# VectorE's side work in the attention takes one input from PSUM, and the PSUM banks are shared out anew

## The chip, the cores and the metric

The kernel runs on one core of one Trainium2 chip. The metric is the device time of one execution in microseconds; the median of three executions of the kernel before is 677.43 us.

## The reference

Three stages follow each other. A linear attention with a decayed state gives `x` (3072 tokens of 384); a router gives each token to one of eight experts, 384 tokens each, in the order of the logits over all tokens; each expert is a two-layer net, and its rows go on through a layer with three weights, a maximum over the three products, and an output weight.

```python
for t in range(S):                                   # attention, B=4, H=8, S=768, D=48
    cur = np.einsum('bhd,bhe->bhde', u[None] * kt, vt)
    y[:, :, t] = np.einsum('bhd,bhde->bhe', rt, state + cur)
    state = w[None, :, :, None] * state + np.einsum('bhd,bhe->bhde', kt, vt)
...
for idx in np.argsort(-logits.flatten()):            # routing, logits = x @ w_gate
    tok, e = (int(idx) // E, int(idx) % E)
    if assigned[tok] >= 0 or counts[e] >= cap:
        continue
    assigned[tok] = e
...
out[mask] = np.maximum(x[mask] @ w1[e], 0.0) @ w2[e] # experts
...
h = np.maximum(np.maximum(x @ w1, x @ w2), x @ w3)   # last layer, weights in float64
return (h @ w_out).astype(np.float32)
```

## The kernel before

The attention is cut into 24 steps (`NT`), one for each of 4 batches and 6 chunks of 128 positions; chunks are the outer loop, so the first four steps have no state yet. `Attention.run` writes the order of the work out by hand, and every engine works its instructions off in that order. In step i it issues: loads for steps i+4 and i+3 on SP's queue; on POOL `decayed(i+2)` (L129), `natural(i+3)` (L184), `bonus(i+2)` (L192, L193); a slot of side work; `turn(i+2)`, four TensorE transposes into the PSUM tile `pT`, which ScalarE copies to `kt` (L213, L215); `fade(i-1)`, four ScalarE scalings of the state `S` (L293); a second slot; `scores(i+1)`, sixteen matmuls into two `pA` tiles, masked to `am` by two VectorE products (L227, L230); `extra(i+1)`, a VectorE sum `bon` and a POOL product `bv` (L201, L203); a third slot; `cross(i-1)`, three transposes of `x` into the PSUM tile `pX`, copied to `xt` by ScalarE, and ScalarE's sum of squares of `x` (L302 to L305); `keep(4)`, four matmuls on constants whose result nobody reads (L237, constant `KEEP`); `rows(i)`, the products with the state and with `am` into two `pY` tiles, added to `bv` as `x` by VectorE (L248, L263); `gate(i-2)`, the logits into the bank `lg` (L313); a fourth slot; and `state(i)`, eight products into the PSUM tile `pK`, to which VectorE adds `S` as `st` (L281, L285).

The side work prepares weights for the later stages while the attention runs. `Feed.take` hands it out by slot: each item has a cost, and a slot's budget is what brings the feed up to the share of the whole cost that is due by then, at most 0.9. Three kinds of items matter here.

- `weight`: four sums of squares of a weight's two loaded blocks on ScalarE (`look`, L628), a scale found from them, then `split(n)`: ScalarE writes the scaled weight rounded to f16 (`upper`, L695), and one item later VectorE subtracts this from the scaled weight for the f16 rest (`lower`, L699). In the attention it runs for both weights of expert 0 (six parts of 512 columns, four of 768), and for the first weight of expert 1 without the rests (`left`).
- `double`: decodes a float64 weight in three blocks of 768 columns to f32 in SBUF. ScalarE writes the magnitude into `da` (L745), VectorE shifts it (`shift`, L760), joins low bits (`low`, L767) and the sign (`sign`, L776), ScalarE squares the result (L628), and after the scale is known `split(j)` halves it as above (ScalarE L801, VectorE L804). It runs for two of the three weights.
- `spread`: the peak over partitions: a transpose of one column (`turn`, L410) in slot 4, a VectorE maximum (L412), a matmul that hands it to all partitions (`share`, L416) in slot 2 of the next step, and five small VectorE operations on it. Both use a fresh `pX`.

The eight PSUM banks are: `lg` 1, `pX` 1, `pT` 1, `pA` 2, `pY` 2, `pK` 1.

```python
            side(1)
            self.turn(i + 2)
            self.fade(i - 1)
            side(2)
            self.scores(i + 1)
            self.extra(i + 1)
            side(3)
            if i < NT - 2:
                self.cross(i - 1)
                self.keep(KEEP)
                self.rows(i)
```

Of the kernel before, what the change touches and what calls it, by code (L numbers as in the profile page):

```python
# [18 lines left out]
C = 128  # L19
# [18 lines left out]
KEEP = 4  # L38
# [6 lines left out]
class Attention:  # L45


    def __init__(self, ctx, tc, K, r, rt, k, v, w, u, wg, x_dram, spare, routing):
# [7 lines left out]
        self.psum = ctx.enter_context(tc.tile_pool(name="psum_a", bufs=1, space=PSUM))  # L56
        self.ST = {}
# [38 lines left out]
        self.bank = self.psum.tile([128, 512], F32, name="lg")  # L96
        self.lg = self.bank[:, :NT * E].rearrange("p (m e) -> p m e", e=E)
# [33 lines left out]
    def tables(self, wcol):  # L131
# [27 lines left out]
        idle = psum.tile([128, 512], F32, name="pX")  # L159
# [111 lines left out]
    def state(self, i):  # L271
# [5 lines left out]
        pk = psum.tile([128, NP, WIDE], F32, name="pK")  # L277
# [18 lines left out]
    def cross(self, i):  # L296
# [3 lines left out]
        px = psum.tile([128, 3, C], F32, name="pX")  # L300
# [92 lines left out]
class Scales:  # L393
# [9 lines left out]
    def spread(self, peak, then):  # L403
# [4 lines left out]
        def turn():  # L408
            p = self.psum()
            nc.tensor.transpose(p[:1, :128], peak() if callable(peak) else peak, self.K.identf)  # L410
            st["m"] = self.tile(shape=(1, 1))
            nc.vector.tensor_reduce(st["m"], p[:1, :128], AX.X, OP.max)  # L412

        def share():
            p = self.psum()
            nc.tensor.matmul(p[:, :1], self.K.onesf[:1, :], st["m"], start=True, stop=True)  # L416
            then(p[:, :1])
# [179 lines left out]
class Experts:  # L597
# [27 lines left out]

    def square(self, x, total):
# [27 lines left out]
    def weight(self, e, which, routed=False, left=False):  # L654
# [37 lines left out]

        def upper(n):
            raw, (hi, _) = part(*parts[n])
            nc.scalar.activation(hi, raw, AF.Copy, scale=st["s"])  # L695

        def lower(n):
            raw, (hi, lo) = part(*parts[n])
            nc.vector.scalar_tensor_tensor(lo, raw, st["s"], hi, op0=OP.mult, op1=OP.subtract)  # L699

        def split(n):
            def go():
                if n < len(parts):
                    upper(n)
                if n and not left:
                    lower(n - 1)
            return go
# [19 lines left out]
    def double(self, i):  # L727
# [14 lines left out]
        def magnitude(j):  # L742
            a = bits[j] = self.wp.tile([128, 768], I32, name="da", bufs=2)
            a = a.bitcast(F32)
# [18 lines left out]
        def low(j):  # L763
            def go():
                if j + 1 < nb:
# [32 lines left out]
        def split(j):  # L798
            def go():
                if j < nb:  # L800
                    nc.scalar.activation(halves(j)[0], st["x"][:, j], AF.Copy, scale=st["s"])  # L801
                if j:
                    hi, lo = halves(j - 1)
                    nc.vector.scalar_tensor_tensor(lo, st["x"][:, j - 1], st["s"], hi, op0=OP.mult, op1=OP.subtract)  # L804
            return go

        near = [[blocks[j]] + blocks[j + 1:j + 2] for j in range(nb)]
        return ([(lambda: magnitude(0), False, blocks[:1], 0.3)] * (not early)
                + [(f(j), False, b, t) for j in range(nb)
                   for f, b, t in ((shift, blocks[j:j + 1] if early else near[j], 0.8), (low, near[j], 1.1), (sign, blocks[j:j + 1], 1.1))]  # L810
# [673 lines left out]
def body(ctx, tc, r, rt, k, v, w, u, wg, w1, w2, v1, v2, v3, wo, out, dbg=None):  # L1484
# [14 lines left out]
    with ExitStack() as actx:  # L1499
        A = Attention(actx, tc, K, r, rt, k, v, w, u, wg, x_dram,  # L1500
                      lambda: X.wp.tile([128, 1536], F32, name="stage", bufs=Feed.SLOTS), routing)
        X.sc.psum = lambda: A.psum.tile([128, 3, C], F32, name="pX").rearrange("p j n -> p (j n)")
# [51 lines left out]
```

## Time and profile before

| what | before |
|---|---|
| median of 3 runs (all) | 677.43 us (676.73, 677.43, 841.12) |
| the profiled execution, its own time | 679.12 us |
| span in the profile | 677.4 us |
| busy PE / VectorE / ScalarE / POOL | 95% / 58% / 52% / 35% |
| mean granted TensorE clock | 0.957 |

The time is what a run measures; the span is from the first to the last instruction of the profiled execution. The attention takes the time from about 11 us to 158.7 us, where ScalarE reads the finished logits; routing follows up to about 200 us, and the experts take the rest. Rows of a timeline give the start in us, the time from the first start to the last end of a merged group, engine, line, operation, written tile and read tiles, shape, and the number of instructions; in square brackets stands the idle time of the engine before it and what ended that.

### The profile page before, as it was taken

The numbers are of one execution on the slowest core, as the hardware profiler recorded it, in microseconds if no ns is written. First come the engines' busy times: TensorE is split into PE (matmuls) and PEld (weight loads), VectorE is DVE, ScalarE is ACT, GpSimd is POOL, SyncE is SP. The second block draws the span as 40 slices with busy tenths as digits, with TensorE's granted clock in tenths as the row PEclk, the third lists the DMA queues.
The fourth block names the chain that finished last, engine by engine and source line by source line (L and its number), as shares of the span: only waits on it lengthen the run. The fifth ranks groups of instructions, "written<-read, shape, count | busy, mean of one in ns | idle before, by whom it ended". The sixth has DMA issues, their size and how long they took to land.

```text
span 677.4 us, 14362 instructions
## 1 busy us (share of the span) xinstructions
PE 642.2 (95%) x5660; PEld 429.9 (63%) x5660; DVE 394.8 (58%) x1027; ACT 350.2 (52%) x782; POOL 238.2 (35%) x268
## 2 busy tenths in 40 slices
PE   6999899998779998999999999999999999999996
PEld 4788787887566664666666666656665666666663
DVE  7777988757745767774556366354626544451321
ACT  3567474854443557574755655546544545332321
POOL 6989999980150003231122023112202111110222
PEclk8889998996579999999999999999999999999999
DMA  8877876625054309064134135112414200000000
GB/s 223 291 233 226 292 223 183 210 81 210 2 156 82 142 3 204 28 125 144 59 117 118 47 129 117 48 59 71 117 47 129 53 30 13 24 1 1 36 1 35
DMA packets 54763, 72.98 MB, mean 108 GB/s; under 512 B 21408, under 2 KB 42016, under 8 KB 54688
## 3 DMA queue, kind: packets, MB, share of 16 engines
q1 hardware_dynamic: 51616, 62.55, 31.3%
q0 software_dynamic: 3072, 9.44, 4.8%
q8 instruction: 46, 0.75, 0.5%
q14 instruction: 29, 0.24, 0.1%
HBM read 58.41 MB, written 9.44 MB: 100 GB/s over the span
## 4 chain that ended last, share of the span: by engine, by line
PE 60%; issue 7%; DVE 2%; POOL 1%; ACT 1%; POOLq 0%; DVEq 0%
PE pg L932 29%; PE ps L932 23%; PE px L1027 8%; POOL gt L1014 1%; DVE top L1009 1%; ACT gt L1013 0%; POOL out_dram L1034 0%; PE px L914 0%; POOLq L1550 0%; DVE da L760 0%; ACT top L1007 0%; ACT x2s L989 0%; ACT junk L628 0%; DVE sc L435 0%; DVE xr L905 0%
## 5 line engine op out<-in xcount | busy, mean ns | idle before, releaser
L932 PE MATMUL pg<-x2s,v 128*128 128x384 f16 x1296 | 217.0, 326 | 2.7 <-ACT top L1007 2.7
L932 PEld LDWEIGHTS <-v 128*128 128x128 f16 x1296 | 126.8, 98 | 86.8 <-issue 3.2
L1014 POOL TENSOR_TENSOR gt<-top,gt 128x384 f16<-128x384 f32 x48 | 44.4, 925 | 341.3 <-ACT gt L1013 291.9
L932 PEld LDWEIGHTS <-w 128*128 128x128 f16 x1242 | 117.2, 99 | 73.1 <-issue 1.6
L1009 DVE SCALAR_TENSOR_TENSOR top<-pg,sc,top 128x384 f32<-128x384 f32 x96 | 59.1, 616 | 75.0 <-PE pg L932 66.2
L932 PE MATMUL ps<-ht,w 128*128 128x384 f16 x576 | 94.9, 326 | 0.0
L699 DVE SCALAR_TENSOR_TENSOR w<-stage,sc,w 128x512 f16<-128x512 f32 (+1 forms) x80 | 70.4, 903 | 41.1 <-ACT w L695 40.8
L932 PE MATMUL ps<-xt,w 128*128 128x384 f16 (+1 forms) x540 | 88.6, 317 | 0.2 <-issue 0.2
L1013 ACT ACTIVATE gt<-top 128x384 f16<-128x384 f32 x48 | 25.0, 522 | 111.6 <-DVE top L1009 109.4
L1027 PE MATMUL px<-wo,gt 128*128 128x384 f16 x432 | 72.2, 326 | 1.8 <-POOL spacer L1033 1.0
L695 ACT ACTIVATE w<-stage,sc 128x512 f16<-128x512 f32 (+1 forms) x80 | 62.0, 797 | 3.0 <-DVE sc L466 1.2
L1027 PEld LDWEIGHTS <-gt 128*128 128x128 f16 x432 | 41.9, 98 | 30.8 <-POOL spacer L1033 1.7
L628 ACT ACTIVATE junk<-stage 128x768 bf16<-128x768 f32 x64 | 53.6, 837 | 6.3 <-DMA stage<-in_moe_w_dram 5.6
L962 DVE SCALAR_TENSOR_TENSOR ht<-ps,ht 128x384 f16<-128x384 f32 x56 | 30.9, 555 | 32.0 <-ACT ht L961 31.9
L1034 POOL DMA_INDIRECT out_dram<-o,ids x24 | 23.8, 993 | 40.8 <-ACT o L1032 40.8
L973 ACT ACTIVATE x<-ps 128x384 f32<-128x384 f32 x24 | 11.8, 490 | 49.7 <-PE ps L932 49.7
L230 DVE TENSOR_TENSOR am<-pA,mask 128x512 f32<-128x512 f32 x48 | 30.8, 682 | 10.3 <-PE pA L227 10.2
L1007 ACT ACTIVATE top<-pg,sc 128x384 f32<-128x384 f32 x48 | 27.7, 576 | 17.6 <-PE pg L932 17.2
L961 ACT ACTIVATE ht<-ps 128x384 f16<-128x384 f32 x56 | 26.7, 481 | 16.1 <-PE ps L932 16.0
L129 POOL TENSOR_TENSOR rt<-rt,tr 128x512 f32<-128x512 f32 x22 | 31.6, 1438 | 1.3 <-DMA rt<-in_rt_dram 1.3
L227 PE MATMUL pA<-rt,kt 64*128 64x128 f32 x384 | 29.9, 295 | 2.0 <-DVE am L230 1.9
L184 POOL TENSOR_TENSOR kp<-kn,tkn 128x384 f32<-128x384 f32 (+1 forms) x25 | 28.3, 1135 | 4.4 <-ACT tkn L168 3.8
(238 smaller groups left out, 851.9 us busy)
## 6 DMA issues: line engine op xcount, KB each, us to landing
stage<-in_moe_w_dram SPq DMA_DIRECT2D x41, 768.0 KB, 5.2
kn<-in_k_dram SPq DMA_DIRECT2D x24, 192.0 KB, 5.0
rn<-in_r_dram SPq DMA_DIRECT2D x24, 192.0 KB, 5.4
v<-in_v_dram SPq DMA_DIRECT2D x24, 192.0 KB, 3.2
rt<-in_rt_dram SPq DMA_DIRECT2D x48, 96.0 KB, 3.5
x_rows<-x SPq DMA_DIRECT2D x24, 192.0 KB, 2.6
stage<-in_moe_w_out_dram SPq DMA_DIRECT2D x3, 768.0 KB, 6.3
xg<-x_rows,ids POOLq DMA_INDIRECT x24, 5.1
```

The source lines that it names most:

```text
L129: (engine or self.nc.gpsimd).tensor_mul(self.RT[i], self.RT[i], self.tr)
L184: self.nc.gpsimd.tensor_mul(self.KN[i][:, heads, :D], kn[:, heads], self.tkn[:, heads, :D])
L227: nc.tensor.matmul(pa[s][:, j, :], kt[FULL[s], j * C:(j + 1) * C], rt[FULL[s], j * C:(j + 1) * C], start=True, stop=True, skip_group_check ...
L230: nc.vector.tensor_mul(am[:, s], pa[s], self.mask[:, None, :].to_broadcast([128, NP, C]))
L628: self.nc.scalar.activation(self.K.junk, x, AF.Square, accum_out=total)
L695: nc.scalar.activation(hi, raw, AF.Copy, scale=st["s"])
L699: nc.vector.scalar_tensor_tensor(lo, raw, st["s"], hi, op0=OP.mult, op1=OP.subtract)
L932: nc.tensor.matmul(p[:, rows], w[:, wi, k, cols], x[:, xi, k, rows], start=k == 0 and wi + xi == 0, stop=k == kb - 1 and xi == 1, skip_gro ...
L962: nc.vector.scalar_tensor_tensor(h[:, 1, f], p, 0.0, h[:, 0, f], op0=OP.max, op1=OP.subtract)
L1009: nc.vector.scalar_tensor_tensor(t, p, self.ratio[i], top, op0=OP.mult, op1=OP.max)
L1014: nc.gpsimd.tensor_sub(gt[:, 1, g], top, gt[:, 0, g])
L1027: nc.tensor.matmul(p, gt[:, gi, g, a * 128:(a + 1) * 128], self.WO[:, wi, g, :], start=g == 0 and gi + wi == 0, stop=g == self.KG - 1 and ...
```

## The change

- A PSUM tile `lane` of two banks is set up once. The bank of `pX` is gone, and the tile `pK` moves into the upper half of the bank `lg` (columns 256 to 511), so that logits, state products, the matmuls of `keep` and, in columns 192 to 255, the result of `share` stand in one bank.
- `cross` and the transpose of `spread` use `pT`, the tile of `turn`. There is one buffer of it.
- In `weight` (not for the `left` one) and in `double`, ScalarE copies each upper half from SBUF (f16) into `lane` (f32) after it has written it, and VectorE's subtraction reads it there. Parts of up to 512 columns take the two banks of `lane` in turn; parts of 768 columns all use the same 768 columns.
- The magnitudes of blocks 1 and 2 of each `double` are written to `lane` in place of SBUF, and shifted, joined and read there. ScalarE's magnitude of the next block is an item of its own (cost 0.3) behind the sign of the block ahead; before, it was issued together with `low` of the block ahead, into another buffer.
- `KEEP` goes from 4 to 2.

```diff
-KEEP = 4
+KEEP = 2
...
+        self.lane = self.psum.tile([128, 1024], F32, name="lane")
...
+        self.spot = self.bank[:, 192:256]
+        self.pk = self.bank[:, 256:].rearrange("p (j n) -> p j n", n=WIDE)
...
-        idle = psum.tile([128, 512], F32, name="pX")
+        idle = self.lane[:, 512:]
...
-        pk = psum.tile([128, NP, WIDE], F32, name="pK")
+        pk = self.pk
...
-        px = psum.tile([128, 3, C], F32, name="pX")
+        px = psum.tile([128, 512], F32, name="pT")[:, :DM].rearrange("p (j n) -> p j n", n=C)
...
         def turn():
-            p = self.psum()
+            p = self.row()
...
         def share():
-            p = self.psum()
+            p = self.spot()
...
+    def twin(self, n, width):
+
+        n = n % 2 * 512 if width <= 512 else 0
+        return self.lane[:, n:n + width]
...
+        apart = self.early and not left
+
+        def copy(n):
+            raw, (hi, _) = part(*parts[n])
+            nc.scalar.activation(self.twin(n, raw.shape[-1]), hi, AF.Copy)
+
         def lower(n):
             raw, (hi, lo) = part(*parts[n])
+            if apart:
+                hi = self.twin(n, raw.shape[-1])
             nc.vector.scalar_tensor_tensor(lo, raw, st["s"], hi, op0=OP.mult, op1=OP.subtract)
...
                 if n and not left:
                     lower(n - 1)
+                if n < len(parts) and apart:
+                    copy(n)
...
         def magnitude(j):
-            a = bits[j] = self.wp.tile([128, 768], I32, name="da", bufs=2)
-            a = a.bitcast(F32)
+            if early and j:
+                a = self.lane[:, :768]
+                bits[j] = a.bitcast(I32)
+            else:
+                bits[j] = self.wp.tile([128, 768], I32, name="da", bufs=2)
+                a = bits[j].bitcast(F32)
...
         def low(j):
             def go():
-                if j + 1 < nb:
+                if j + 1 < nb and not early:
                     magnitude(j + 1)
...
                 if j:
                     hi, lo = halves(j - 1)
+                    if early:
+                        hi = self.twin(0, 768)
                     nc.vector.scalar_tensor_tensor(lo, st["x"][:, j - 1], st["s"], hi, op0=OP.mult, op1=OP.subtract)
+                if j < nb and early:
+                    nc.scalar.activation(self.twin(0, 768), halves(j)[0], AF.Copy)
...
+                   for f, b, t in [(size, near[j], 0.3)] * (early and j > 0)
+                   + [(shift, near[j], 0.8), (low, near[j], 1.1), (sign, blocks[j:j + 1], 1.1)]]
...
+        X.sc.row, X.sc.spot, X.lane = lambda: A.psum.tile([128, 512], F32, name="pT"), lambda: A.spot, A.lane
```

On ScalarE, where the first `double`'s result is split (`v` is the f16 weight, `kt` and `xt` the copies of `turn` and `cross`), the kernel before has:

```order
L801 ACTIVATE v_82<-wo,sc_1626 128x768 [waits DVE_49]
L304 ACTIVATE xt<-pX 128x384 [waits PE_49]
L305 ACTIVATE junk,norms<-x 128x384 [waits Activation_49]
L801 ACTIVATE v_82<-wo,sc_1626 128x768 x2
L215 ACTIVATE kt_111<-pT 128x512 [waits PE_49]
```

The changed kernel has at the same place:

```order
L823 ACTIVATE v_82<-wo,sc_1593 128x768 [waits DVE_49]
L830 ACTIVATE lane<-v_82 128x768 [waits Activation_49]
L307 ACTIVATE xt<-pT 128x384 [waits PE_49]
L308 ACTIVATE junk,norms<-x 128x384
L823 ACTIVATE v_82<-wo,sc_1593 128x768
L830 ACTIVATE lane<-v_82 128x768 [waits DVE_49,Activation_49]
L823 ACTIVATE v_82<-wo,sc_1593 128x768
L830 ACTIVATE lane<-v_82 128x768 [waits DVE_49,Activation_49]
L218 ACTIVATE kt_112<-pT 128x512 [waits PE_49]
```

Three copies into `lane` have come in ahead of `kt`, and the second and third wait for VectorE. The order of VectorE at this place is the same in both kernels but for the operand:

```order
L266 TENSOR_TENSOR x<-pY,bv 128x4x48 [waits DMAHW2_49,PE_49,Pool_49]
L266 TENSOR_TENSOR x<-pY,bv 128x4x48 [waits PE_49]
...
L828 SCALAR_TENSOR_TENSOR v_82<-wo,sc_1593,lane 128x768 [waits DVE_49,Activation_49]
L288 TENSOR_TENSOR st<-lg,S_117 128x192 [waits PE_49]
L828 SCALAR_TENSOR_TENSOR v_82<-wo,sc_1593,lane 128x768 [waits Activation_49] x2
L233 TENSOR_TENSOR am<-pA,mask 128x512 [waits PE_49] x2
```

The subtraction stands behind `x`, `st` and ahead of `am`, and now reads `lane`.

On TensorE, the kernel before has in one step of the steady part:

```order
L213 MATMUL pT<-identf,kp_115 128x128 [waits Activation_49,Pool_49]
L213 MATMUL pT<-identf,kp_115 128x128 x3
...
L302 MATMUL pX<-identf,x 128x128 [waits DVE_49,Activation_49]
L302 MATMUL pX<-identf,x 128x128 x2
L237 LDWEIGHTS onesf
L237 MATMUL lg<-onesf 128x256
L237 LDWEIGHTS onesf
L237 MATMUL lg<-onesf 128x256
```

and the changed kernel:

```order
L216 MATMUL pT<-identf,kp_114 128x128 [waits Activation_49,Pool_49]
L216 MATMUL pT<-identf,kp_114 128x128 x3
...
L305 MATMUL pT<-identf,x 128x128 [waits DVE_49,Activation_49]
L305 MATMUL pT<-identf,x 128x128 x2
L240 LDWEIGHTS onesf
L240 MATMUL lg<-onesf 128x256 [waits DVE_49]
```

Both kinds of transposes now write `pT`, so that the wait of `cross` for ScalarE is one for the `kt` copy of the same step, and that of `turn` one for the `xt` copy of the step ahead; before, each waited for the copy of its own tile one step earlier. The matmuls of `keep` wait for VectorE's `st`, which reads their bank.

## Rows read from the trace of the kernel before

**Rows 1.** Windows: TensorE, weight loads, VectorE, ScalarE, POOL busy (instructions), clock, DMA share, GB/s.

```profile
80.00:100.00 20.00, 19.53 (x410) 16.71 (x407) 17.70 (x34) 14.17 (x39) 19.76 (x16) 1.00 0.75 241
```

**Rows 2.** Timeline of one step of the attention, TensorE and ScalarE.

```profile
64.03 0.69 PE L281 MATMUL pK<-v,kp 128*64 128x64 f32 x16
...
64.64 0.66 PE L213 MATMUL pT<-identf,kp 128*128 128x128 f32 x4
...
65.33 0.60 ACT L215 ACTIVATE kt<-pT 128x512 f32<-128x512 f32 x1 [0.96 <-PE pT L213]
...
65.83 1.00 ACT L293 ACTIVATE S<-st,w 128x48 f32<-128x48 f32 x4
...
66.32 0.55 PE L302 MATMUL pX<-identf,x 128*128 128x128 f32 x3
...
66.70 0.60 PE L237 MATMUL lg<-onesf 128*128 128x256 bf16 x4
...
67.23 0.69 PE L248 MATMUL pY<-S,rt 64*64 64x64 f32 x32
...
68.94 0.83 PE L313 MATMUL lg<-wg,xt 128*128 128x8 f32 x6
...
69.70 0.69 PE L281 MATMUL pK<-v,kp 128*64 128x64 f32 x16
```

**Rows 3.** Timeline of POOL: two successive products `rt`, twice.

```profile
65.92 1.98 POOL L129 TENSOR_TENSOR rt<-rt,tr 128x512 f32<-128x512 f32 x1
...
73.69 1.58 POOL L129 TENSOR_TENSOR rt<-rt,tr 128x512 f32<-128x512 f32 x1
...
141.58 1.27 POOL L129 TENSOR_TENSOR rt<-rt,tr 128x512 f32<-128x512 f32 x1
...
146.60 1.27 POOL L129 TENSOR_TENSOR rt<-rt,tr 128x512 f32<-128x512 f32 x1
```

**Rows 4.** Timeline of TensorE where it waits inside the attention.

```profile
77.00 0.66 PE L213 MATMUL pT<-identf,kp 128*128 128x128 f32 x4 [0.92 <-POOL kp L184]
...
79.41 0.52 PE L302 MATMUL pX<-identf,x 128*128 128x128 f32 x3 [0.66 <-DVE x L263]
...
100.84 0.69 PE L281 MATMUL pK<-v,kp 128*64 128x64 f32 x16
103.29 0.66 PE L213 MATMUL pT<-identf,kp 128*128 128x128 f32 x4 [1.76 <-POOL kp L184]
...
109.89 0.69 PE L281 MATMUL pK<-v,kp 128*64 128x64 f32 x16
```

**Rows 5.** Windows, TensorE alone: busy (instructions), granted clock, DMA share, GB/s.

```profile
105.00:106.00 1.00, 1.00 (x8) 0.50 0.52 93
```

**Rows 6.** Groups by line and shape, first 300 us: count, busy us, mean ns, idle before.

```profile
L230 DVE TENSOR_TENSOR am<-pA,mask 128x512 f32<-128x512 f32 x48 | 30.8, 682 | 10.3 <-PE pA L227 10.2
...
L767 DVE SCALAR_TENSOR_TENSOR da<-stage,da 128x768 int32<-128x768 int32 x12 | 14.9, 1244 | 0.2
...
L760 DVE TENSOR_SCALAR da<-da 128x768 int32<-128x768 int32 x12 | 8.0, 665 | 6.6 <-ACT da L745 6.6
L801 ACT ACTIVATE v<-wo,sc 128x768 f16<-128x768 f32 x9 | 7.9, 929 | 0.0
...
L804 DVE SCALAR_TENSOR_TENSOR wo<-gt,sc,wo 128x768 f16<-128x768 f32 x3 | 2.9, 1013 | 1.4 <-ACT wo L801 1.4
```

**Rows 7.** Timeline of VectorE where the first `double` is split.

```profile
94.56 0.62 DVE L263 TENSOR_TENSOR x<-pY,bv 128x192 f32<-128x192 f32 x2 [0.94 <-POOL rt L129]
95.10 1.20 DVE L804 SCALAR_TENSOR_TENSOR v<-wo,sc,v 128x768 f16<-128x768 f32 x1
...
96.49 3.15 DVE L804 SCALAR_TENSOR_TENSOR v<-wo,sc,v 128x768 f16<-128x768 f32 x2
```

**Rows 8.** Timeline of TensorE: the first peak's transpose waits for ScalarE.

```profile
32.28 0.27 PE L410 MATMUL pX<-identf,sc 128*1 128x128 f32 x1 [1.43 <-ACT xt L304]
```

**Rows 9.** Timeline of ScalarE: a square that waits for VectorE, ahead of `kt`.

```profile
73.14 0.84 ACT L628 ACTIVATE junk<-wo 128x768 bf16<-128x768 f32 x1 [4.60 <-DVE wo L776]
```

More of the change, by code (lines that the diff above doesn't have):

```diff
@@ L803, in go, with size @@
                     hi, lo = halves(j - 1)
+                    if early:
+                        hi = self.twin(0, 768)
                     nc.vector.scalar_tensor_tensor(lo, st["x"][:, j - 1], st["s"], hi, op0=OP.mult, op1=OP.subtract)
+                if j < nb and early:
+                    nc.scalar.activation(self.twin(0, 768), halves(j)[0], AF.Copy)
             return go
         near = [[blocks[j]] + blocks[j + 1:j + 2] for j in range(nb)]
-        return ([(lambda: magnitude(0), False, blocks[:1], 0.3)] * (not early)
+        def size(j):
+            return lambda: magnitude(j)
+        near = [blocks[j:j + 1] for j in range(nb)] if early else near
+        return ([(size(0), False, blocks[:1], 0.3)] * (not early)
                 + [(f(j), False, b, t) for j in range(nb)
-                   for f, b, t in ((shift, blocks[j:j + 1] if early else near[j], 0.8), (low, near[j], 1.1), (sign, blocks[j:j + 1], 1.1))]
+                   for f, b, t in [(size, near[j], 0.3)] * (early and j > 0)
+                   + [(shift, near[j], 0.8), (low, near[j], 1.1), (sign, blocks[j:j + 1], 1.1)]]
                 + [(last, False, [], 0.1 if early else 1.05)] + self.scaled(st, column, powers, [])
@@ L1501, in body @@
                       lambda: X.wp.tile([128, 1536], F32, name="stage", bufs=Feed.SLOTS), routing)
-        X.sc.psum = lambda: A.psum.tile([128, 3, C], F32, name="pX").rearrange("p j n -> p (j n)")
+        X.sc.row, X.sc.spot, X.lane = lambda: A.psum.tile([128, 512], F32, name="pT"), lambda: A.spot, A.lane
         A.run(feed, lambda most: X.rest(most))
```

## The prediction

> **What bounds the kernel now.** I read the windows of the attention first, since only there does the change touch anything; then one step in order of time on TensorE; then POOL and the waits of TensorE; last the groups by shape. In the window from 80 to 100 us three engines are nearly full: TensorE 19.53 of 20 us, POOL 19.76, VectorE 17.70 [rows 1]. Which of them sets the pace shows in one step: from one start of `pK` to the next are 69.70 - 64.03 = 5.67 us, and every group of matmuls starts as the one ahead ends, so TensorE waits for nothing [rows 2]. POOL is as fast only where VectorE leaves it alone: two `rt` products lie 146.60 - 141.58 = 5.02 us apart late in the attention, when there is little side work, and 73.69 - 65.92 = 7.77 us apart in its midst, where one product took 1.98 us in place of 1.27 [rows 3]. VectorE is stretched too: a 768-column operation with both tensors in SBUF takes 1.24 us on average (`low`) and 1.01 where POOL has nothing to do (the last row), while `am`, with one tensor in PSUM, took 30.8 / 48 = 0.64 us throughout [rows 6]. So the two hold each other up, and where POOL or VectorE falls behind, TensorE waits: 0.92 us for `kp` and 0.66 us for `x` near 77 us, 1.76 us for `kp` near 103 us, after which the granted clock was 0.50, the lower of its two levels (1.2 GHz), and the whole step took 109.89 - 100.84 = 9.05 us [rows 4, 5]. TensorE's own 5.67 us is the floor; contention lifts some steps above it. After the attention nothing changes in the order, so a gain there moves everything behind it by as much.
>
> **The change part by part.**
>
> *Two matmuls of `keep` less.* Four take 67.23 - 66.70 = 0.53 us of TensorE's time [rows 2], so two less give 0.265 us in each step that TensorE sets. I count 18 (steps 4 to 21; earlier ones wait for other things): 18 x 0.265 = 4.8 us. It is zero where something else ends last. The floor becomes 5.40 us, still above POOL's 5.02.
>
> *Contention gone.* 24 VectorE operations of the side work (10 `lower`, 6 in the splits of `double`, 4 `low`, 4 `sign`) now have one tensor in PSUM. The trace has no such operation of 768 columns. From above it is bounded by 1.24 us (no gain), from below by the rate of `am`, 0.64 x 768 / 512 = 0.96 us [rows 6]; I take 0.96, as `am` is the nearest row, with one tensor on either side. In the split of the first `double`, where two took 3.15 us [rows 7], that is 0.6 us less for each. The four shifts that move to PSUM may go the other way, from 0.67 us at most to the same 0.96, 1.2 us in all, covered by what the others give back. POOL's products fall back to 1.27 us and the like. What TensorE gets of this are the waits it had: 0.92 + 0.66 us, and 9.05 - 5.67 = 3.38 us for the step with the low clock [rows 4]. Sum 5.0 us; nothing if the contention stays.
>
> *ScalarE's copies.* Sixteen are added, six of 512 columns and ten of 768. Bounds for 768 columns: 0.74 us, from `kt`, whose 512 columns out of PSUM hold ScalarE 65.83 - 65.33 = 0.50 us [rows 2], and 0.93, the scaled write of `v` [rows 6]. I take 0.75, the row without a scale by column. As work alone they are hidden, as ScalarE has 14.17 of 20 us [rows 1]. The Trainium skill (ScalarE: Activation LUTs, What ACT_TABLE_LOAD costs) gives 186 ns + 0.833 ns per element for an ACTIVATE without pointer operands; by that an estimated 0.83 us, and each of the two waits of the next part would be 0.16 us longer. No run here shows a copy into PSUM.
>
> *The new waits.* All 768-column copies use one place, so a copy waits until VectorE has read the one ahead, and behind it on ScalarE stands `kt`; `cross`, now in the same PSUM tile, waits for `kt`. In the splits of the two `double`s the chain goes: from the end of `pY` (68.94 in a plain step) VectorE's `x` 0.54 us (95.10 - 94.56 [rows 7]), subtraction 0.96, copy 0.75, subtraction 0.96, copy 0.75, `kt` 0.55, and some 0.2 for the hand-overs: 4.7 us. TensorE wants to start `cross` after `gate` (69.70 - 68.94 = 0.76) and after 66.32 - 64.03 = 2.29 us of `pK`, `pT` and `pA`: 3.05 us [rows 2]. It waits 1.65 us, twice: 3.3 us. The split of the 768-column weight has a shorter chain from the start of `pK`: its 0.69, about 0.3 for `st`, subtraction 0.96, copy 0.75, `kt` 0.55, 3.25 in place of 2.29 us, so `cross` waits 0.95. In that step `xt` too stands behind a copy, whose subtraction is queued behind the two `am` (1.28 us) that came later by this wait; I estimate that the next `turn` waits 0.8 us for it. Together 1.75 us. In the 512-column weight two places are used in turn, and `kt` is ready as before. All this is between zero (`kt` never last) and twice as much (subtractions at 1.24 us and every one late).
>
> *`share` and `keep` in one bank with the state.* `keep` waits for `st`, which ends over half a microsecond earlier. `share` waits for `st` as well, and where `low` stands ahead of `st` on VectorE I expect 0.6 us; 1.2 us over the five, between 0 and 3. At the first peak the transpose waited 1.43 us [rows 8]; the matmuls ahead of it now come later by about what `cross` and `keep` wait for `kt` and the four scalings (1.00 us in [rows 2]), so this wait shrinks to about 1.0, and `share` then waits about 1.4 for the scalings of its step. Between no change and 2.2 us of gain if the clock stays up there; I take 0.5 us of gain.
>
> *Clock.* A wait of 1.76 us was followed by the lower level, at a cost beyond the wait of 9.05 - 5.67 - 1.76 = 1.6 us [rows 4, 5]; waits of 0.92 and 0.66 us were not. Of the two waits of 1.65 us I count one as followed by it: 1.6 us, between 0 and 3.2.
>
> The sum: -4.8 - 5.0 + 3.3 + 1.75 + 1.2 - 0.5 + 1.6 = -2.5 us. Against the profiled execution (679.12 us, of which the span is 677.4) this is 676.6; that execution lies 1.7 us above the median of 677.43, so I forecast 677.43 - 2.5, about 675.
>
> **The rivals.**
>
> *No new wait is ever last.* Then only the gains stand, and the start keeps its clock: -4.8 - 5.0 - 2.2 = -12.0 us, 665.4 us. For it: VectorE gets faster, and `kt` was on time in most steps, with ScalarE idle 0.96 us ahead of it [rows 2]. Against: the chain above follows from the order, and leaves ScalarE no way around.
>
> *The clock falls at each new wait (slower).* The place is `cross` behind `kt` in the splits, and the point from which it decides is a wait of about 1.4 us: 1.43 [rows 8] and 1.76 [rows 4] are the waits that I hold against it. If four waits (both `double`s, two in the 768-column weight) each cost 1.65 + 1.6 = 3.25 us, they come to 13.0 in place of 3.3 + 1.75 + 1.6, 6.35 more: +3.9 us, 681.3. For it: two `keep` matmuls fewer to fill the gaps; ScalarE already stood 4.60 us for VectorE ahead of one `kt` [rows 9], harmless while `cross` had a tile of its own and a TensorE wait now. Against: VectorE lags less without contention.
>
> *Contention stays.* If one tensor in PSUM doesn't free POOL, the 5.0 us are not won: +2.5 us, 679.9. Against it stands `am` at 0.64 us whatever POOL does, against 1.24 and 1.01 for two tensors in SBUF [rows 6]. I give this rival little for that. The Trainium skill (SBUF — State Buffer, SBUF: two separate sides) has VectorE and GpSimd lock a shared port pair for a whole instruction, by VectorE when it reads two tensors in SBUF; by that rule the new operations don't take it and the gain is whole, and the trace's 1.98 against 1.27 us agrees.
>
> **How the numbers follow.** The forecast has 0.5, no new wait 0.17, the falling clock 0.18, contention that stays 0.12, and 0.03 is for what I haven't seen. The range takes in the second half of the first rival's way and the whole of the other two: 668 to 681 us. A measurement of this kernel tells about 2%, 13.5 us, from no change. Faster by that much would need every gain and more than the 12.0 us counted: 0.03. Slower by that much would need the lower clock through much of the attention: 0.04. Within: 0.93.
>
> **What would show it.** Right: steps of 5.4 us from `pK` to `pK` in the middle; POOL's `rt` near 1.27 us nearly everywhere; VectorE's subtractions of 768 columns near 0.96 us; waits of TensorE in `cross` for ScalarE's `kt`, of 1 to 2 us, in the two splits of `double` and that of the 768-column weight; the logits read some 2 to 3 us earlier than 158.7 us. Wrong: POOL's products still at 1.7 to 2 us; `cross` waiting in steps without splits; the lower clock over more than two or three steps; or a difference that arises after the attention.

## The result: 0.7% slower, and the profile after

Seven-tenths of a per cent slower, where I had forecast four-tenths faster: the changed kernel takes 681.65 us in the median (680.66 to 684.2, six runs), the kernel before 677.43 beside it (five runs), a ratio of 1.0069 with an interval of [1.0047, 1.0091]. Three executions far slower than their fellows (841.12 us of the kernel before, 938.16 and 752.30 us of the first experiment below) stand in no ratio and in no median from here on. The profiled execution took 681.25 us (span 679.5), 2.1 us more than that of before, and all of that and a little more has arisen by the time the logits are read: 161.54 us against 158.68. So the place is the attention, as foreseen; the sign of the sum was wrong.

The window that answers to [rows 1] (TensorE, weight loads, VectorE, ScalarE, POOL busy, clock, DMA share, GB/s):

```profile
80.00:100.00 20.00, 18.25 (x354) 15.45 (x352) 14.99 (x33) 14.05 (x35) 18.12 (x18) 1.00 0.71 223
```

VectorE has 2.7 us less to do and POOL 1.6, and POOL's `rt` takes 1.33 us on average between 40 and 158 us where it took 1.48, so most of the contention went. Yet TensorE is *less* busy by 1.3 us: something new is last. A plain step, which answers to [rows 2] (the state's product is now `lg<-v,kp`):

```profile
73.46 0.69 PE L284 MATMUL lg<-v,kp 128*64 128x64 f32 x16
...
76.14 0.38 PE L240 MATMUL lg<-onesf 128*128 128x256 bf16 x2
76.45 0.69 PE L251 MATMUL pY<-S,rt 64*64 64x64 f32 x32
...
78.92 0.69 PE L284 MATMUL lg<-v,kp 128*64 128x64 f32 x16
```

It takes 5.46 us in place of 5.67: `keep` holds TensorE 76.45 - 76.14 = 0.31 us, not half of 0.53. The groups that answer to [rows 6], over the first 300 us:

```profile
L828 DVE SCALAR_TENSOR_TENSOR v<-wo,sc,lane 128x768 f16<-128x768 f32 x6 | 6.1, 1010 | 3.2 <-ACT lane L830 3.2
...
L830 ACT ACTIVATE lane<-v 128x768 f32<-128x768 f16 x6 | 4.9, 815 | 2.1 <-DVE v L828 2.1
...
L782 DVE TENSOR_SCALAR da<-da 128x768 int32<-128x768 int32 x8 | 4.5, 565 | 6.8 <-ACT da L767 6.8
...
L782 DVE TENSOR_SCALAR lane<-lane 128x768 int32<-128x768 int32 x4 | 3.8, 958 | 0.6 <-ACT lane L767 0.6
L789 DVE SCALAR_TENSOR_TENSOR lane<-stage,lane 128x768 int32<-128x768 int32 x4 | 3.8, 957 | 0.1
```

VectorE's operations with one tensor in PSUM take 0.96 to 1.01 us, close to the 0.96 of the forecast. To the right of the bar stands what is new: VectorE waits for ScalarE's copy (3.2 us over six) and the copy for VectorE (2.1 us). They take turns over one place. What that does to TensorE is in its waits, which answer to [rows 4] and [rows 8]:

```profile
32.16 0.27 PE L413 MATMUL pT<-identf,sc 128*1 128x128 f32 x1 [1.23 <-ACT xt L307]
...
35.09 0.58 PE L419 MATMUL lg<-sc,onesf 1*128 1x1 f32 x2 [1.45 <-ACT S L296]
...
45.06 0.55 PE L305 MATMUL pT<-identf,x 128*128 128x128 f32 x3 [1.13 <-ACT kt L218]
...
63.62 0.55 PE L305 MATMUL pT<-identf,x 128*128 128x128 f32 x3 [1.20 <-ACT kt L218]
...
68.64 0.63 PE L216 MATMUL pT<-identf,kp 128*128 128x128 f32 x4 [1.18 <-ACT xt L307]
...
91.70 0.38 PE L419 MATMUL lg<-sc,onesf 1*128 1x1 f32 x2 [0.31 <-DVE st L288]
...
100.65 0.55 PE L305 MATMUL pT<-identf,x 128*128 128x128 f32 x3 [2.01 <-ACT kt L218]
...
133.59 0.55 PE L305 MATMUL pT<-identf,x 128*128 128x128 f32 x3 [2.01 <-ACT kt L218]
```

From 40 us on no wait is for POOL any more; nearly all are for ScalarE's `kt` and `xt`: the splits of the 512-column weight (45 us), of the 768-column weight (64 and 69) and of the two `double`s (101 and 134). The last but one of these waits in all three engines, in order of time:

```profile
95.47 0.92 ACT L823 ACTIVATE v<-wo,sc 128x768 f16<-128x768 f32 x1
95.67 0.62 DVE L266 TENSOR_TENSOR x<-pY,bv 128x192 f32<-128x192 f32 x2 [0.72 <-PE pY L251]
96.22 1.00 DVE L828 SCALAR_TENSOR_TENSOR v<-wo,sc,lane 128x768 f16<-128x768 f32 x1
...
97.31 0.81 ACT L830 ACTIVATE lane<-v 128x768 f32<-128x768 f16 x1 [0.92 <-DVE v L828]
98.06 0.92 ACT L823 ACTIVATE v<-wo,sc 128x768 f16<-128x768 f32 x1
98.16 1.01 DVE L828 SCALAR_TENSOR_TENSOR v<-wo,sc,lane 128x768 f16<-128x768 f32 x1 [0.67 <-ACT lane L830]
99.27 0.81 ACT L830 ACTIVATE lane<-v 128x768 f32<-128x768 f16 x1 [0.28 <-DVE v L828]
100.02 0.58 ACT L218 ACTIVATE kt<-pT 128x512 f32<-128x512 f32 x1
```

Read it downwards: subtraction, copy, subtraction, copy, then `kt`, and at 100.65 the token transposes, for which TensorE had been ready since `pA` ended, at 97.47 + 1.16 = 98.63. Behind this wait the clock fell; the rows that answer to [rows 5] are TensorE's groups around it and the same window:

```profile
95.51 0.83 PE L316 MATMUL lg<-wg,xt 128*128 128x8 f32 x6
96.27 0.69 PE L284 MATMUL lg<-v,kp 128*64 128x64 f32 x16
...
97.47 1.16 PE L230 MATMUL pA<-rt,kt 64*128 64x128 f32 x16
...
105.01 1.12 PE L284 MATMUL lg<-v,kp 128*64 128x64 f32 x16
...
107.11 2.08 PE L230 MATMUL pA<-rt,kt 64*128 64x128 f32 x16
...
112.29 0.69 PE L284 MATMUL lg<-v,kp 128*64 128x64 f32 x16
```

```profile
105.00:106.00 1.00, 1.00 (x17) 0.50 0.17 66
```

`pA` takes 2.08 us in place of 1.16. The steps from `lg<-v,kp` to the next one, 96.27 to 105.01 and 105.01 to 112.29 us, are 8.74 and 7.28 us long: beyond the plain step and the wait that is 1.27 + 1.82 = 3.1 us. The second wait of 2.01 us was not followed by a fall.

The account of the profiled execution up to the logits: `keep` 18 x 0.21 = -3.8, contention -5.0, the new waits for `kt` and `xt` (with 0.21 us for the fade at 45.8) +7.7, `share` at 91.70 +0.3, half clock +3.1, and +0.7 ahead of the state's product that starts at 41.56 us (40.87 in before), where the waits of 1.23 and 1.45 us and the half clock (34 to 41 us) cost more than the one wait of 1.43 us and the half clock behind it (33 to 39 us) in before. That is +3.0; 161.54 - 158.68 = 2.9 us was measured. The medians lie 4.2 us apart and the profiled executions only 2.1, since that of before was 1.7 us above its median and this one 0.4 below. The profiled execution of before was not a usual one: its mean granted clock of 0.957 lies below each of the 75 executions of before that were recorded beside the experiments (0.958 to 0.971). What is priced from its waits, the -5.0 us, may be more than a usual execution has to give.

### The profile page after: what moved, and what is told of

Same layout as the page of the kernel before. It is cut to its first block, busy times and chain, and to the rows that moved or that the text cites. A ratio compares the mean times of both kernels' runs of the same rounds, so it can differ in the third digit from the quotient of the medians.

```text
span 679.5 us, 14301 instructions
## 1 busy us (share of the span) xinstructions
PE 640.1 (94%) x5616; PEld 427.4 (63%) x5616; DVE 386.2 (57%) x1027; ACT 361.9 (53%) x798; POOL 224.5 (33%) x268
## 4 chain that ended last, share of the span: by engine, by line
PE 60%; issue 7%; DVE 2%; POOL 1%; ACT 1%; POOLq 0%; DVEq 0%
PE pg L963 29%; PE ps L963 23%; PE px L1058 8%; POOL gt L1045 1%; DVE top L1040 1%; ACT gt L1044 0%; POOL out_dram L1065 0%; PE px L945 0%; POOLq L1581 0%; DVE da L782 0%; ACT top L1038 0%; ACT x2s L1020 0%; ACT junk L636 0%; DVE sc L438 0%; DVE xr L936 0%
## 5 line engine op out<-in xcount | busy, mean ns | idle before, releaser
L715 DVE SCALAR_TENSOR_TENSOR w<-stage,sc,w 128x512 f16<-128x512 f32 (+1 forms) x70 | 59.0, 864 | 41.1 <-ACT w L705 40.8
L132 POOL TENSOR_TENSOR rt<-rt,tr 128x512 f32<-128x512 f32 x22 | 29.1, 1321 | 1.5 <-DMA rt<-in_rt_dram 1.5
L1063 ACT ACTIVATE o<-px,sc 128x384 f32<-128x384 f32 x24 | 13.9, 579 | 28.8 <-PE px L1058 21.5
```

Source lines behind the costliest of these rows:

```text
L132: (engine or self.nc.gpsimd).tensor_mul(self.RT[i], self.RT[i], self.tr)
```

## The experiments

**Theory.** The copies wait for VectorE, `kt` and `xt` stand behind them on ScalarE, and because the transposes share a bank TensorE waits for ScalarE. **Rivals.** ScalarE simply has too much work; the shared banks cost by themselves; taking two `keep` matmuls away loses the clock. Each kernel was compared with runs of the kernel before on the same chip. Their medians there were 677.25 us (for the four kernels behind the changed one in the table), 676.64 (for the next four) and 676.95 (for the last four), so it is the ratios that compare one row with another:

| kernel | median, us | ratio to before, interval |
|---|---|---|
| changed kernel | 681.65 | 1.0069 [1.0047, 1.0091] |
| turn ahead of the first slice | 682.47 | 1.0073 [1.0053, 1.0094] |
| changed, `KEEP` 4 | 683.21 | 1.0096 [1.0069, 1.0122] |
| before, `KEEP` 2 | 676.46 | 0.9993 [0.9981, 1.0005] |
| before, transposes in one bank | 678.03 | 1.0030 [1.0006, 1.0054] |
| doubles' splits in SBUF | 676.41 | 1.0002 [0.9985, 1.0019] |
| every other copy, doubles | 676.87 | 0.9994 [0.9978, 1.0010] |
| transposes in banks of their own | 678.58 | 1.0029 [1.0009, 1.0048] |
| reordered | 678.54 | 1.0017 [0.9996, 1.0038] |
| no copies, magnitudes in SBUF | 677.94 | 1.0011 [0.9994, 1.0028] |
| every other copy everywhere | 670.37 | 0.9908 [0.9880, 0.9936] |
| the same, `share` out of the logits' bank | 668.75 | 0.9867 [0.9844, 0.9889] |
| the same, `KEEP` 4 | 670.25 | 0.9892 [0.9872, 0.9913] |

### The parts one by one

**Turn ahead of the first slice of side work**, so that `kt` is not behind the copies:

```diff
-            side(1)
             self.turn(i + 2)
+            side(1)
             self.fade(i - 1)
```

> The changed kernel with one edit of its order: turn(i + 2) is issued ahead of the first slot of side work, so that on ScalarE kt no longer stands behind that slot's copies. Theory (cross waits for kt, kt for a copy, the copy for VectorE's subtraction): the waits of cross of 2.01, 2.01, 1.20 and 1.13 us in the changed kernel mostly go, and with them the 3 us of low clock near 105 us; 7 to 9 us less than the changed kernel, 673 to 675 us, faster than the kernel before. The turn that waits 1.18 us for xt stays. Rival (ScalarE has too much work): the wait moves to the state's scalings or to xt, under 2 us won. Rival (the clock, for want of keep): the low clock stays, under 2 us won.

It came out at 682.47 us, with the ratio of the changed kernel: a miss. The waits for `kt` are gone, all of them, but TensorE's rows show others:

```profile
57.69 0.63 PE L216 MATMUL pT<-identf,kp 128*128 128x128 f32 x4 [1.08 <-DVE sc L415]
...
71.51 0.63 PE L216 MATMUL pT<-identf,kp 128*128 128x128 f32 x4 [2.54 <-ACT xt L307]
```

Three tenants use the bank `pT` in turn (keys, tokens, peaks). The waits of 1.20 and 1.18 us at the 768-column weight became one of 2.54, now for `xt`, at the peaks the turn waits for VectorE's reading (1.08, 1.05 and 0.42 us), and `keep` once waits 1.28 us for the fade. The low clock stayed too: the granted clock was 0.50 from 73 to 76 us and from 97 to 103 us. Moving one reader forward only passes the wait to the next.

**Four `keep` matmuls in the changed kernel**, and **two in the kernel before**:

```diff
-KEEP = 2
+KEEP = 4
```

> The changed kernel with four matmuls of keep in place of two. Theory: TensorE sets the pace in the steps without a wait, so each of some 18 steps becomes 0.21 us longer (5.46 to 5.67): 3 to 4 us slower than the changed kernel, about 685 us. Rival (the loss is the clock, for want of keep): the low clock near 105 us goes and the kernel gets 2 to 4 us faster, 678 to 680 us.

```diff
-KEEP = 4
+KEEP = 2
```

> The kernel before with two matmuls of keep in place of four and nothing else. Theory: 0.21 us less in each step that TensorE sets, part of it taken back where POOL's contention sets the step: 2 to 4 us faster than before, 673.5 to 675.5 us. Rival (the clock needs four): more low clock in the profile, and no gain or a loss.

In the changed kernel the two matmuls are worth 1.6 us between the medians (1.8 by the ratios, whose intervals overlap), under half of 3.8. Part of the rest is the clock. With four, TensorE waits 2.02 us for `kt` in the split of the first `double`. The state's products around it:

```profile
99.22 0.69 PE L284 MATMUL lg<-v,kp 128*64 128x64 f32 x16
...
108.47 0.69 PE L284 MATMUL lg<-v,kp 128*64 128x64 f32 x16
...
114.16 0.69 PE L284 MATMUL lg<-v,kp 128*64 128x64 f32 x16
```

One step is 9.25 us long and the next 5.69, plain again. Beyond the plain step of 5.68 us and the wait, that is 1.55 us, where the changed kernel lost 3.1 in two steps. So the rival of the clock doesn't explain the loss, for with four the kernel got no faster; but of these two executions the one with two matmuls more lost half as much to the low clock.

In the kernel before they are worth nothing that these runs tell from zero, against the 2 to 4 us of the theory. Its windows and waits show one reason:

```profile
60.00:80.00 20.00, 17.19 (x315) 14.44 (x313) 19.57 (x27) 12.36 (x34) 19.77 (x16) 0.92 0.77 248
```

```profile
101.77 0.66 PE L213 MATMUL pT<-identf,kp 128*128 128x128 f32 x4 [2.07 <-POOL kp L184]
```

POOL is busy for 19.77 of 20 us. A shorter step of TensorE makes it wait for `kp`: the row is the longest of nine such waits from 44 to 132 us, 8.8 us together, against four of 3.2 us in the kernel before from 40 us on. A second reason is on record, and these runs don't separate the two: the mean granted clock of a whole execution was 0.960 over these twelve and 0.966 over 23 of the kernel before, as it was 0.955 over the six of the changed kernel and 0.962 over its six with four `keep` matmuls. In which stage the untraced executions lost it is not known. Either way the `keep` term does not simply add to the others; I had added it to the relief of POOL as if the two were independent.

**The kernel before with the token transposes and the peak's transpose in `pT`**, nothing else:

```diff
-        px = psum.tile([128, 3, C], F32, name="pX")
+        px = psum.tile([128, 512], F32, name="pT")[:, :DM].rearrange("p (j n) -> p j n", n=C)
...
-            p = self.psum()
+            p = self.row()
```

> The kernel before with the transposes of cross and of the peak in the PSUM tile of turn, and nothing else; no copies, no lane. Theory: sharing the tile makes TensorE wait wherever kt is late on ScalarE, which in the kernel before was so four times behind a square that waits for VectorE (kt 1.8 to 3.0 us late): waits of 0.8 to 2.5 us in cross, 5 to 9 us slower than before with the low clock that follows, 683 to 687 us. Rival (the shared tile costs nothing by itself, the copies do): within 1.5 us of before.

The ratio is 0.3% over before, less than expected, and the twelve runs are spread from 675.92 to 686.04 us, five of them over 680. The profiled run is the longest, and shows the mechanism without any copy, on ScalarE and TensorE:

```profile
71.59 0.84 ACT L628 ACTIVATE junk<-wo 128x768 bf16<-128x768 f32 x1 [4.81 <-DVE wo L776]
...
72.43 0.58 ACT L215 ACTIVATE kt<-pT 128x512 f32<-128x512 f32 x1
...
73.06 0.55 PE L302 MATMUL pT<-identf,x 128*128 128x128 f32 x3 [2.75 <-ACT kt L215]
```

Here it is the sum of squares that stands for VectorE's decoding, the very wait of [rows 9], and with the shared bank TensorE pays 2.75 us for it. The bank couples TensorE to whatever ScalarE has in hand ahead of `kt`. How often an execution falls into this, only its times tell.

### The copies

**The doubles' splits in SBUF again**, six of the ten 768-column copies gone:

```diff
-                    if early:
-                        hi = self.twin(0, 768)
...
-                if j < nb and early:
-                    nc.scalar.activation(self.twin(0, 768), halves(j)[0], AF.Copy)
```

> The changed kernel (681.65 us, 4.1 over before) with one part undone: the six subtractions of the two doubles' splits read the upper half from SBUF again, and the six 768-column copies are not made. Theory (the copies make the wait: the second and third copy stand on ScalarE until VectorE has read the one 768-column place, kt is queued behind them, and the token transposes need kt's bank): the two 2.01 us waits of the token transposes go, and with them the 3.1 us of half clock behind the first; VectorE against GpSimd in SBUF comes back for six instructions, at most 1.8 us (the 1.76 us wait for kp at 103.29 in before). Sum -4.0 -3.1 +1.5, so 676 us (674 to 678). Rival (sharing the bank alone, with any side work ahead of kt): token transposes still wait 1.5 to 2.8 us at these places, 680 us or more.

**Every other copy of the doubles**, four of six:

```diff
-                    if early:
+                    if early and j % 2:
                         hi = self.twin(0, 768)
...
-                if j < nb and early:
+                if j < nb and early and j % 2 == 0:
```

> The changed kernel with copies for the first and third block of each double only (four instead of six); the middle block's subtraction reads SBUF, so that no copy stands until VectorE has read the block before. Theory (it is the copy's wait for the one place, not its 0.82 us): the two token-transpose waits fall from 2.01 to 0.6 us or less, the clock does not fall behind the first: 681.65 -2.8 -3.1 +0.5 = 676 us (674.5 to 678). Rival (ScalarE's own time, 0.94 + 0.82 per block): the waits stay over 1.2 us and the time over 679.

Both came out as the theory said, 676.41 and 676.87 us, by the ratios 4.5 and 5.1 us below the changed kernel, and no wait of TensorE for POOL's `kp` came back after 40 us. Without the six copies the waits of 2.01 us in the splits are gone (one of 0.79 us is left a step later, behind a sum of squares). With four copies, each 0.82 us of ScalarE's time as before, one wait of 0.32 us is left in the splits (the traced execution, 673.85 us, was 3.0 below its median):

```profile
126.57 0.55 PE L305 MATMUL pT<-identf,x 128*128 128x128 f32 x3 [0.32 <-ACT kt L218]
```

Taking away two copies of six does nearly what taking away all six does. So it is not ScalarE's load, but the copy that must wait until the one place has been read.

**Transposes in banks of their own**, for which the copies keep one bank (512 columns only; magnitudes in SBUF):

```diff
-        self.lane = self.psum.tile([128, 1024], F32, name="lane")
+        self.lane = self.psum.tile([128, 512], F32, name="lane")
...
-        px = psum.tile([128, 512], F32, name="pT")[:, :DM].rearrange("p (j n) -> p j n", n=C)
+        px = psum.tile([128, 512], F32, name="pX")[:, :DM].rearrange("p (j n) -> p j n", n=C)
```

> The changed kernel with the token transposes and the peak's transpose in a bank of their own again. For it the copies keep one bank: only the 512-column subtractions read PSUM, the 768-column ones and the magnitudes are in SBUF as before; two keep-warm matmuls, and the state's product in the logits' bank, stay. Theory (the waits come from the shared transposes' bank): no wait of TensorE for kt or xt is left anywhere after 40 us, so -6.7 us of waits and -3.1 of clock; the waits for kp come back, as with two keep-warm matmuls alone in the kernel before (8.8 us of them, total 676.46 us). 676 us (674 to 678). Rival (the state's product, the share and the keep-warm matmuls in one bank cost as much): waits for S and st of over 3 us, 680 us.

Half a miss: no wait for `kt` is left, as the theory said, but the time is 678.58 us. Nor does the run tell the bank from the copies, since the 768-column copies are gone with it. Waits for `kp` are few. What stands out is the clock: from 34 us on it was half over much of two steps (8.66 and 7.37 us from one start of `pA` to the next), and near 92 us it fell after short waits, which made that step 8.26 us long (TensorE's rows, then the window):

```profile
90.57 0.66 PE L216 MATMUL pT<-identf,kp 128*128 128x128 f32 x4 [0.47 <-POOL kp L187]
91.65 0.57 PE L419 MATMUL lg<-sc,onesf 1*128 1x1 f32 x2 [0.42 <-DVE st L288]
92.15 2.08 PE L230 MATMUL pA<-rt,kt 64*128 64x128 f32 x16
```

```profile
92.00:100.00 8.00, 8.00 (x111) 0.59 0.61 198
```

**Reordered**: `kt` and the fade ahead of the first slice, `xt` ahead of the third, the peak in the copies' free columns:

```diff
-            side(1)
             self.turn(i + 2)
             self.fade(i - 1)
-            side(2)
+            side(1)
             self.scores(i + 1)
             self.extra(i + 1)
-            side(3)
+            side(2)
             if i < NT - 2:
                 self.cross(i - 1)
+                side(3)
...
-        X.sc.row, X.sc.spot, X.lane = lambda: A.psum.tile([128, 512], F32, name="pT"), lambda: A.spot, A.lane
+        X.sc.row, X.sc.spot, X.lane = lambda: A.lane[:, 896:], lambda: A.spot, A.lane
```

> The changed kernel with all its PSUM copies, written in another order: the turn (kt) and the state's fade stand ahead of the first slice of side work, the token transposes (xt) ahead of the third, and the peak's transpose is in the copies' free columns. On ScalarE kt has no side work between it and the fade of the step before, and xt only two slices. Theory: waits for kt, xt and sc fall under 0.5 us each, 7 us less in all, and the clock's 3.1 us go with them: 672 us (670 to 675), below both kernels. Rival (what the turn alone ahead of the first slice showed, 683.7 us: the side work's time on ScalarE comes out at whichever bank is next): the waits turn up at the fade (keep-warm matmuls, share) or at xt, 680 us or more.

The rival's mechanism held, though not its 680 us: 678.54, by the ratios 3.5 us below the changed kernel. The waits of 2.01 us are gone, but `keep` in the logits' bank now waits for VectorE's reading of `share`, five times for 0.68 to 1.22 us, and `kt` still stands behind the side work of the step before:

```profile
57.94 0.38 PE L240 MATMUL lg<-onesf 128*128 128x256 bf16 x2 [1.22 <-DVE sc L463]
...
70.31 0.55 PE L305 MATMUL pT<-identf,x 128*128 128x128 f32 x3 [0.88 <-ACT kt L218]
```

**No copies at all**, magnitudes in SBUF: `keep` and the shared banks alone.

```diff
-        apart = self.early and not left
+        apart = False
...
-            if early and j:
-                a = self.lane[:, :768]
-                bits[j] = a.bitcast(I32)
```

> The changed kernel without any PSUM copy and with the magnitudes in SBUF: two keep-warm matmuls, the state's product in the logits' bank and the shared transposes' bank alone. It tells what the copies and magnitudes in PSUM are worth by themselves. Theory (kt and xt are held up by whatever side work ScalarE has in hand, here the sums of squares that wait for VectorE's contended decoding, as in the kernel before with the shared bank): 1.0 to 2.8 us of waits for kt at the doubles' decoding and waits for kp as in the kernel before: 679 us (677 to 683), slower than with half the copies. Rival (the copies only cost): 675 us or less.

677.94 us, as expected, though not for all the reasons given: from 60 us on only one wait for `kt` (0.58 us) is there, and six for `kp` come to 6.4 us, of which this is the longest:

```profile
115.01 0.99 PE L216 MATMUL pT<-identf,kp 128*128 128x128 f32 x4 [1.88 <-POOL kp L187]
```

So the tensors in PSUM do take the contention off POOL, and the full set of copies then costs more than it frees: 1.0069 against 1.0011. The shared banks cost little by themselves: 1.0011 against the 0.9993 of before with `KEEP` 2, with intervals that overlap, and 1.0030 for the bank of the transposes with `KEEP` 4.

### A version below both

**Every other copy everywhere**: as in the doubles, in both weights too.

```diff
-            if apart:
-                hi = self.twin(n, raw.shape[-1])
+            if apart and n % 2 == 0:
+                hi = self.twin(0, raw.shape[-1])
...
-            nc.scalar.activation(self.twin(n, raw.shape[-1]), hi, AF.Copy)
+            nc.scalar.activation(self.twin(0, raw.shape[-1]), hi, AF.Copy)
...
-                if n < len(parts) and apart:
+                if n < len(parts) and apart and n % 2 == 0:
                     copy(n)
```

> The changed kernel with every second copy only, in the weights' splits too (3 of 6 in the 512-column weight, 2 of 4 in the 768-column weight, 4 of 6 in the doubles; the others read SBUF). The doubles alone gave 676.87 us. Theory (a copy that stands behind VectorE's reading of the one place holds kt and xt up): the 2.37 us of waits for kt and xt at the 768-column weight (62.72 and 67.75 us) and the 1.93 us for kt at the 512-column weight (43.0 us, with its half clock of 1.5 us) fall to 0.5 us each or go; the share's 1.45 us behind the state's fade stays. 676.87 - 3.5 = 673.4 us (671.5 to 675.5). Rival (ScalarE's own work per block sets the end): the waits stay over 1 us each, 676 to 678 us.

670.37 us, 1.1 below the range given. In the split of the first double, where the changed kernel waited 2.01 us, ScalarE now runs through (its rows, with the VectorE operation that reads the first copy):

```profile
88.38 0.94 ACT L823 ACTIVATE v<-wo,sc 128x768 f16<-128x768 f32 x1
89.34 0.81 ACT L830 ACTIVATE lane<-v 128x768 f32<-128x768 f16 x1
...
90.97 1.75 ACT L823 ACTIVATE v<-wo,sc 128x768 f16<-128x768 f32 x2
91.71 1.01 DVE L828 SCALAR_TENSOR_TENSOR v<-wo,sc,lane 128x768 f16<-128x768 f32 x1
92.81 0.82 ACT L830 ACTIVATE lane<-v 128x768 f32<-128x768 f16 x1
93.56 0.58 ACT L218 ACTIVATE kt<-pT 128x512 f32<-128x512 f32 x1
```

No row has a wait in brackets: two scaled writes stand between the copies, and the place has just been read when the second copy starts (91.71 + 1.01 = 92.72 against 92.81). The margin is under a tenth of a microsecond. On TensorE, from the start of `gate` to the token transposes are 94.20 - 91.00 = 3.20 us, where they were 100.65 - 95.51 = 5.14:

```profile
91.00 0.83 PE L316 MATMUL lg<-wg,xt 128*128 128x8 f32 x6
...
94.20 0.55 PE L305 MATMUL pT<-identf,x 128*128 128x128 f32 x3
```

**The same, with the broadcast of `share` in the copies' free columns**, and **that with four `keep` matmuls**:

```diff
-... lambda: A.spot, A.lane
+... lambda: A.lane[:, 960:], A.lane
```

> As the run before it, and the share's broadcast goes to the copies' free columns instead of the logits' bank, where the state's product is. Theory: the 1.45 us wait of TensorE for ScalarE's fade at the first share (34 us) and the 0.3 to 0.8 us for the state's sum at the third (91 us) go, and the half clock behind the first with them (about 1.5 us): 2 to 3 us under the run before it, 671 us (669 to 674). Rival (the share then waits for VectorE's maximum, which is as late): within 0.5 us of the run before it.

> As the run before it, with four keep-warm matmuls per step instead of two. Measured in the traces 0.53 us for four and 0.31 for two, 0.21 us per step. Theory (with GpSimd at 0.8 of its time instead of 0.99, TensorE's own work sets the step): 18 x 0.21 = 3.8 us slower than the run before it, less what a wait of 1 us keeps of the clock: +3 us (+1.5 to +4). Rival (the two matmuls taken away fall into idle time, as in the kernel before, where it gave 0.5 us): under 1 us.

668.75 us, a ratio of 0.9867 [0.9844, 0.9889] to before: the lowest of all. The 1.45 us of `share` behind the fade are gone and one wait of 1.07 us for `xt` took their place. The step is worth 1.6 us by the medians and 2.8 by the ratios, whose intervals just overlap, so the 2 to 3 expected are neither shown nor refuted. TensorE is busy for 119.47 of the 122 us from 28 to 150:

```profile
28.00:150.00 122.00, 119.47 (x2315) 102.89 (x2314) 97.72 (x204) 89.71 (x231) 109.02 (x103) 0.99 0.70 223
```

Two more `keep` matmuls cost 1.5 us there by the medians and 1.7 by the ratios (the intervals 0.9892 [0.9872, 0.9913] and 0.9867 [0.9844, 0.9889] overlap), at the low end of what the theory gave; the mean granted clock was again the higher with four, 0.968 against 0.964.

## Why the prediction was wrong, by its own steps

- **Contention gone (-5.0): right.** TensorE's waits for `kp` and `x` went, and the shift in PSUM rose to 0.96 us as bounded. The subtractions take 1.01 us, not 0.96: I had divided `am`'s busy time by its count, and the mean of one in the same row, 682 ns, gives 1.02 us by column, as does the last row of [rows 6], 1.01, without contention. Without the tensors in PSUM 6.4 us of waits for `kp` are there.
- **`keep` (-4.8): too large.** A step got 0.21 us shorter, not 0.265: -3.8 in the steps, and 1.5 to 1.8 us where it was undone. I had halved a group of matmuls whose first two cost more than the next two.
- **ScalarE's copies: size off.** 0.815 us, not 0.75. I took the row of `kt` by column; the estimate from the Trainium skill (ScalarE: Activation LUTs, What ACT_TABLE_LOAD costs), 0.83 us, was the nearer one.
- **The new waits (+3.3 + 1.75 = 5.05): the step that failed.** The chain was right link by link, and its length from the end of `pY` was 5.14 us against 4.7 (two subtractions and two copies longer by 0.05 and 0.06 us each, and some 0.2 us in hand-overs): 2.01 us twice, not 1.65. The 768-column weight waited 1.20 + 1.18 = 2.38, not 1.75. And for the 512-column weight I said that `kt` is ready as before: it made TensorE wait 1.13 us, and the fade behind it another 0.21; ScalarE had worked there since 40.21 us, when a copy had waited 1.75 us for VectorE, with one pause of 0.23. Together 7.7 us. That they come from the copies is shown: without the doubles' six, or with every other one, the time falls by 4.5 and 5.1 us, and with every other one in the weights too no wait for `kt` over 0.5 us is left.
- **Clock (+1.6): undersized.** One of the two long waits was followed by the lower level, as I had counted, but for nearly two steps: 3.1 us.
- **`share` and `keep` in one bank: 0.3 us, not 1.2**, and the start 0.7 us dearer instead of 0.5 cheaper; I had counted in part on the clock staying up there, and in the 1.45 us wait of `share`, foreseen at 1.4, it fell.

The terms were off by 1.0 (`keep`), 2.7 (waits), 1.5 (clock), 1.2 (start) and -0.9 (`share`), 5.5 us in all; the attention of the traced execution came out 2.9 + 2.5 = 5.4 us from the sum. The rival of the falling clock gave 681.3 us (just above the 681 at which the range ended, though the range was to take in the whole of it), next to what was measured, but in the traced execution not for its reason: it wanted a fall at each of four waits, and there was one among them. There it was more waiting. For the other five executions of the changed kernel the share of the clock stays open: their mean granted clock was 0.949 to 0.962, where the executions of before have 0.965 on average, and the traced pair, 0.960 against 0.957, doesn't show this difference.

What stays open is how much of the saving from `keep` the clock takes back in a usual execution, and what decides whether the clock falls. Runs of one kernel differ by up to 10 us (before with the shared bank), and only one execution of each was traced.

## What to carry to other kernels

A buffer that two engines hand back and forth through one place puts each on the other's clock, and whatever stands behind on either queue pays: copy only as many blocks as leave each copy's place free when its turn comes. Here half of the copies beat all of them by 1.6% and none by 1.0% (the ratios 0.9908, 1.0069 and 1.0011 to before). Before tiles are put into one bank, look at what stands ahead of each tile's *reader* on its engine; a wait that is harmless while a bank is private ([rows 9]) becomes TensorE's. And don't add a saving on one engine to the relief of another as if they were independent: two matmuls less were worth nothing that could be measured while POOL was at 19.8 of 20 us, and the granted clock was lower without them.

## What the runs showed of the hardware that I had not expected

The granted clock does not follow the length of a wait alone. A wait of 2.01 us was followed by 0.50 at 102 us and by no fall at 134 us in the same execution; at the wait of 1.45 us for the fade it fell to 0.50 in the changed kernel, and at one of 1.46 us in the same place not at all in the kernel with every other copy of the doubles (1.00 from 34 to 43 us); in the kernel with banks of its own waits of 0.47 and 0.42 us, 1.1 us apart, were followed by most of a step at half speed (`pA` 2.08 us in place of 1.16), while a wait of 1.93 us for `kt` in the kernel with every other copy of the doubles was followed by a step of only 7.07 us beyond the wait (from one start of `pA` to the next), in place of 5.46. And an operation that works in place on one tensor, the shift, is slower in PSUM than in SBUF: 958 ns against 565 for the same 768 columns.
